# Clustered attention and two mixers: pair 1's raw rows fetched with pair 0's, another order of the set-up

## The chip, the cores and the metric

One core of one Trainium2 chip. The metric is the device time of one execution, in microseconds (us); a table below gives the runs. The engines are PE (matmul), PEld (its weight loads), DVE, ACT, POOL and SP; SP and ACT also issue DMAs, each on a queue of its own (SPq, ACTq in the rows).

## The reference

```python
q_assign = np.argmax(np.einsum('bhsd,hcd->bhsc', q_n, c_n), axis=-1)   # 16 clusters; k_assign likewise
mask = q_assign[:, :, :, None] == k_assign[:, :, None, :]
scores = np.where(mask, scale * np.matmul(q, k.transpose(0, 1, 3, 2)), -1e9)
attn = softmax(scores)                    # over the last axis
x = attn @ v                              # 2 batches, 8 heads, 768 rows, head size 64
# then two mixers on x (2, 768, 512):
#  u = x + (x^T U V)^T ; x = u + relu(u w1) w2          U: 768x32, w1: 512x2048
#  u = x + (relu(x^T T1) T2)^T ; out = u + relu(u w1) w2  T1: 768x256, w1: 512x1536
```

## The kernel before

The attention runs over 8 pairs (2 batches x 4 pairs of heads). A pair's q and k rows are a block of 128 partitions (two heads of 64, a = 0 and 1) by 768 positions, loaded raw into Rq and Rk. From them come a high part (rounded, Hq, Hk) and a low part (the rest), which DMAs stack into the operands qS and kS: "hi" (the high part), "lo" (the low part) and "mask", the rows that the cluster choice gives, so that one matmul adds scores and mask. `cross` (L250) issues the two DMAs of each stack that change partitions.

The cluster choice of a pair: PE multiplies the raw rows with the normalised centroids zc (`scores`), DVE transposes the result out of PSUM (`scores_out`, L198), then an argmax in steps arg0 (L206), arg1, arg2 (L219), arg3, arg4 (L229) and `mask_rows` (L232), on DVE or partly on POOL.

A pair has 12 tiles, 96 in all. Tile n takes, in `step`: the score matmuls of tile n+2 (`s_mm`, 4 matmuls into two PSUM banks), their row maximum on DVE (`s_max`, L292), the exponential on ACT (`s_exp`, L297), six PE transposes (`t_mm`, L314) and their evacuation (`t_out`, L319 or L321) into the blocks `pt`, and, from step 7 on, the products with v (`pv`). `ident` is the 128x128 identity. The order of the program on each engine is written out by hand: lists `mid`, `low`, `acts` and `late` say what else is issued in a step, and each engine works strictly in the order written. A DMA that has to wait stops those behind it on its queue.

All matmuls have line L73 (the helper `mm`), all roundings on ACT L78, the subtractions L85. Ahead of the loop stands `setup`: it loads the centroids (L390, L391), pair 0's raw rows (L392, L393) and v (L186), normalises the centroids (L412 to L421), transposes them (L423, copies L425), rounds pair 0's q and k for a = 0 and 1 (L435 to L440, low part of q L438), and does pair 0's cluster choice and masks (L442 to L452); then it loads pair 1's raw rows into Rq and Rk (`load_pair`, L444), rounds them (`q_hi`, `k_hi`), stacks them, does tiles 0 and 1's scores and maxima, pair 1's cluster scores and low parts (L461 to L466). The rest of pair 1's choice follows in steps 0 to 5, its masks in step 6. `load_uv` (L474) loads U and V of the first mixer in step 3; ACT takes U's magnitude (L96, `uv`) in step 11, V's in step 13. Behind the attention come the mixers, almost all PE work.

Of the kernel before, what the change touches and what calls it, by code (L numbers as in the profile page):

```python
# [10 lines left out]
F32R = mybir.dt.float32r  # L11
# [4 lines left out]
ALU = mybir.AluOpType  # L16
# [8 lines left out]
def tile_cluster_attention__then__two_mixers(  # L25
# [49 lines left out]
    def rnd(eng, o, i, scale=1.0):  # L75

        if eng is act:
            act.activation(o, i, AF.Copy, scale=scale)  # L78
        elif eng is dve and scale == 1.0:
            dve.tensor_copy(o, i)  # L80
        else:
            eng.tensor_scalar(out=o, in0=i, scalar1=scale, scalar2=1.0, op0=ALU.mult, op1=ALU.mult)

    def sub(eng, o, a, b):
        eng.tensor_tensor(out=o, in0=a, in1=b, op=ALU.subtract)  # L85
# [90 lines left out]
    wcl = const.tile([P, 16], BF16, name="wcl")  # L176
    msk = const.tile([P, 2], F32, name="msk")

    def load_pair(g, eng=sp):
        b, p = divmod(g, NPAIR)  # L180
        eng.dma_start(Rq, qT[b, p])
        eng.dma_start(Rk, kT[b, p])

    def load_v(g):
        b, p = divmod(g, NPAIR)
# [1 line left out]

    held = {}

    def scores(g):  # L190
        p = g % NPAIR
        held["sc"] = bk = ring()
        for qd in range(4):
            src = (Rq, Rk)[qd // 2]
            mm(ps[32 * qd : 32 * qd + 32, bk, 0:HS], zc[:, ts(p, 32)], src[:, ts(qd % 2, HS)], True, True)

    def scores_out():
        dve.transpose(out=am1, in_=ps[:, held["sc"], 0:HS])  # L198

    v1 = am1.rearrange("p (g c) -> p g c", c=16)  # L200
    v2 = am2.rearrange("p (g c) -> p g c", c=16)
# [29 lines left out]
    def mask_rows(eng):  # L231
        eng.tensor_scalar(out=om, in0=ohT, scalar1=msk[:, 0:1], scalar2=msk[:, 1:2], op0=ALU.add, op1=ALU.mult)  # L232

    def q_hi():
        rnd(act, Hq.bitcast(F32R), Rq, 0.125)

    def k_hi():
        rnd(act, Hk.bitcast(F32R), Rk)

    def q_lo(eng, o):  # L240
        eng.scalar_tensor_tensor(out=o.bitcast(F32R), in0=Rq, scalar=0.125, in1=Hq, op0=ALU.mult, op1=ALU.subtract)

    def k_lo(eng, o):
        sub(eng, o.bitcast(F32R), Rk, Hk)

    def rows(a):
        m, x = 64 * a, 64 * (1 - a)
# [4 lines left out]
        for i in range(2):  # L252
            eng.dma_start(o[x, 1 - i, :], src[m.start + 32 * i : m.start + 32 * i + 32])

    def stack(g, a, what, eng, Lq=Rq, Lk=Rk):
        q, k = f32(qS[g % NST][a]), f32(kS[g % NST][a])
        m, _, y = rows(a)
        if what == "hi":
            eng.dma_start(q[m, :, :], Hq[m].unsqueeze(1).to_broadcast([64, 2, S]))
            eng.dma_start(k[m, 1, :], Hk[m])  # L260
            cross(k, Hk, a, eng)
        elif what == "lo":
            eng.dma_start(k[m, 0, :], Lk[m])
            cross(q, Lq, a, eng)
        else:
            e = eng if type(eng) is tuple else (eng, eng)
            for h in range(2):
                e[h].dma_start(q[y, 0, ts(h, HS)], om[32 * h + 16 * a : 32 * h + 16 * a + 16])
                e[1 - h].dma_start(k[y, 0, ts(h, HS)], om[64 + 32 * h + 16 * a : 80 + 32 * h + 16 * a])
# [34 lines left out]
    def ring():  # L304

        banks.append(banks.pop(0))
        return banks[-1]
# [78 lines left out]
    def setup():  # L386
        with tc.tile_pool(name="tmp", bufs=1) as tmp:
            cc = tmp.tile([P, 2, D], F32, name="cc")
            tiny = tmp.tile([P, 1], F32, name="tiny")
            act.dma_start(cc[:, 0, :], cen)  # L390
            sp.dma_start(cc[:, 1, :], cen)  # L391
            sp.dma_start(Rq, qT[0, 0])  # L392
            act.dma_start(Rk, kT[0, 0])  # L393
            load_v(0)
            make_identity(nc, ident)
            dve.memset(zc, 0.0)
            for t in (qS, kS):
                for i in range(NST):
                    (dve, pool)[i].memset(f32(t[i][1])[32:64], 0.0)
            wi = tmp.tile([P, 16], F32, name="wi")  # L400
            pool.iota(wi, pattern=[[-1, 16]], base=16, channel_multiplier=0, allow_small_or_imprecise_dtypes=True)
            dve.memset(msk[0:64, 0:1], 0.0)
            dve.memset(msk[0:64, 1:2], 1.0)
            dve.memset(msk[64:128, 0:1], -1.0)
            dve.memset(msk[64:128, 1:2], BIG)


            sq = tmp.tile([P, D], F32, name="sq")
            n2 = tmp.tile([P, 1], F32, name="n2")
            n1 = tmp.tile([P, 1], F32, name="n1")  # L410
            nr = tmp.tile([P, 1], F32, name="nr")
            dve.tensor_tensor(out=sq, in0=cc[:, 0, :], in1=cc[:, 0, :], op=ALU.mult)  # L412
            dve.tensor_reduce(out=n2, in_=sq, axis=AX.X, op=ALU.add)
            dve.tensor_scalar(out=n2, in0=n2, scalar1=2.0 ** -100, scalar2=None, op0=ALU.max)
            act.activation(n1, n2, AF.Sqrt)
            dve.reciprocal(nr, n1)
            dve.tensor_tensor(out=nr, in0=nr, in1=n2, op=ALU.mult)
            dve.tensor_tensor(out=n1, in0=n1, in1=nr, op=ALU.add)
            dve.tensor_scalar(out=n1, in0=n1, scalar1=0.5, scalar2=1e-6, op0=ALU.mult, op1=ALU.add)
            dve.reciprocal(nr, n1)  # L420
            dve.tensor_scalar(out=cc, in0=cc, scalar1=nr, scalar2=None, op0=ALU.mult)  # L421
            ct = ps[:, 6, 0:P]
            pe.transpose(ct, cc.rearrange("p a d -> p (a d)"), ident)  # L423
            for a in range(2):
                dve.tensor_copy(  # L425
                    zc[64 * a : 64 * a + 64, :].rearrange("p (h j) -> p h j", j=32)[:, :, 16 * a : 16 * a + 16],
                    ct[64 * a : 64 * a + 64].rearrange("p (h j) -> p h j", j=32)[:, :, 16 * a : 16 * a + 16],
                )
            dve.tensor_copy(wcl, wi)

            l = p32[0]
            for a in range(2):
                m, _, _ = rows(a)
                q, k = qS[0][a], kS[0][a]
                rnd(act, q[m], Rq[m].unsqueeze(1).to_broadcast([64, 2, S]), 0.125)  # L435
                rnd(act, k[m, 1, :], Rk[m])
                sub(pool, k[m, 0, :], Rk[m], f32(k[m, 1, :]))
                dve.scalar_tensor_tensor(out=l[m].bitcast(F32R), in0=Rq[m], scalar=0.125, in1=f32(q[m, 0, :]), op0=ALU.mult, op1=ALU.subtract)  # L438
                cross(f32(k), f32(k[:, 1, :]), a, (act, sp)[a])
                cross(f32(q), l, a, sp)  # L440
            act.activation(tiny, n1, AF.Exp, scale=0.0)
            scores(0)  # L442
            scores_out()
            load_pair(1)  # L444
            arg0()
            arg1(dve)
            arg2()
            arg3(dve)
            arg4()
            mask_rows(dve)  # L450
            for a in range(2):
                stack(0, a, "mask", (act, sp))  # L452
            q_hi()
            k_hi()
            for a in range(2):
                stack(1, a, "hi", sp)
            s_mm(0)
            s_mm(1)
            s_max(0)
            s_max(1)  # L460
            scores(1)  # L461
            scores_out()
            q_lo(dve, Rq)
            k_lo(pool, Rk)
            for a in range(2):
                stack(1, a, "lo", sp)  # L466


    x_ = xn[:, 1].rearrange("p a b c -> p (a b c)")
# [100 lines left out]
    for g in range(G):  # L570
        s0 = NTT * g
        for h in range(2):
            s = s0 + 2 * NT * h + 4 * NT + 1
            at(mid, s, lambda q=2 * g + h: merge(q))
            at(late, s, lambda q=2 * g + h: merge_out(q))
        n, s1 = g + 1, s0
        if 2 <= n < G:
            at(late, s1 - 8 if n > 2 else 1, lambda g=n: load_pair(g))
            at(low, s1 - 3, lambda g=n: scores(g))
            at(acts, s1 - 5, q_hi)  # L580
            at(acts, s1 - 3, k_hi)
            for s, f in ((-3, scores_out), (-2, arg0), (-1, lambda: q_lo(dve, Rq)),
                         (-1, lambda: arg1(pool)), (-1, lambda: k_lo(pool, Rk)), (3, arg2), (3, lambda: arg3(pool)),
                         (5, arg4), (5, lambda: mask_rows(pool))):
                at(late, s1 + s, f)
            for what, s in (("hi", -2), ("lo", 1), ("mask", 7)):
                for a in range(2):
                    at(late, s1 + s, lambda g=n, a=a, w=what: stack(g, a, w, sp))
        if n < G:
            at(late, s1 + 6 if n > 1 else 4, lambda g=n: load_v(g))  # L590
# [6 lines left out]
    for t in range(NS):  # L597
# [5 lines left out]

        at(mid, s, za)
        at(late, s if s == 69 else s + 1, lambda t=t: zadd_out(0, t, held["za"]))
    for s, f in ((0, arg0), (1, lambda: arg1(pool)), (2, arg2), (3, lambda: arg3(pool)), (4, arg4), (5, lambda: mask_rows(pool))):
        at(late, s, f)
    for a in range(2):
        at(late, 6, lambda a=a: stack(1, a, "mask", sp))
    at(late, 3, load_uv)  # L610
    for i, s0, ss in ((0, 11, (12, 12, 12, 12)), (1, 13, (14, 16, 18, 20))):
        at(acts, s0, uv[i][0])
        for f, s in zip(uv[i][1:], ss):
# [360 lines left out]
```

## Time and profile before

| | us |
|---|---|
| median of 3 runs | 769.07 |
| lowest, highest | 767.74, 770.06 |
| the profiled execution | 767.95 |
| its span, first to last instruction | 766.2 |
| PE busy | 738.7 (96%) |
| DVE, ACT, POOL busy | 467.1, 310.1, 166.4 |

The times in rows are us from the start of the span, taken from one profiled execution. A busy PE isn't PE at its peak, since matmuls are pipelined. The page's row of granted clock shows full speed for all 40 slices; the durations in the first 23 us show another pace, so of those the durations are read.

### The profile page before, as it was taken

Reading aid. Unit: us, or ns where it says so; the run is one execution under the profiler, and the core shown is the slowest. Engines: PE = TensorE matmul, PEld = TensorE weight load, DVE = VectorE, ACT = ScalarE, POOL = GpSimd, SP = SyncE. Lnnn points to the kernel's source line nnn. Section 1 sums busy time; section 2 is a strip of 40 time slices with the busy share of each in tenths; the row PEclk is TensorE's granted clock in tenths of the full one; section 3 lists DMA queues with packets and bytes.
Section 4 is the critical chain, followed back from the end, with each engine's and each line's share of the span. In section 5 each row is a group of like instructions: output and inputs, shape, how many; then the busy total and the mean of one; then the engine's idle time right before and its main releaser. Section 6 shows DMA issues by size and latency. Waiting matters only on the chain.

```text
span 766.2 us, 10466 instructions
## 1 busy us (share of the span) xinstructions
PE 738.7 (96%) x3845; PEld 582.1 (76%) x3845; DVE 467.1 (61%) x689; ACT 310.1 (40%) x565; POOL 166.4 (22%) x147
## 2 busy tenths in 40 slices
PE   1899999999999999999999999999999999999998
PEld 0667766766666688888888888888888888888886
DVE  6778988877777366875758587666675432122113
ACT  3777877867776343332232324323232311111010
POOL 3321432421310122321322122125211410000000
PEclk9999999999999999999999999999999999999999
DMA  5886777875311344753632699967885647555652
GB/s 152 191 185 185 179 186 188 243 183 134 87 63 55 112 165 151 287 193 138 220 131 89 222 346 368 337 238 259 283 286 215 214 144 274 192 192 195 243 192 83
DMA packets 51714, 149.38 MB, mean 195 GB/s; under 512 B 7792, under 2 KB 15984, under 8 KB 49616
## 3 DMA queue, kind: packets, MB, share of 16 engines
q1 hardware_dynamic: 51152, 148.01, 59.7%
q10 hardware_dynamic: 512, 0.72, 0.3%
q8 instruction: 30, 0.49, 0.3%
q14 instruction: 20, 0.16, 0.1%
HBM read 97.32 MB, written 32.51 MB: 169 GB/s over the span
## 4 chain that ended last, share of the span: by engine, by line
PE 92%; DVE 3%; DMA 2%; ACT 2%; issue 1%; SPq 0%; ACTq 0%; DVEq 0%
PE ps L73 82%; PE ps L314 7%; DVE nm L292 1%; DMA xn<-in_U_dram 1%; ACT p L297 1%; ACT qk L78 1%; PE ps L377 1%; PE ps L822 1%; PE ps L334 1%; DMA sq__81<-in_qT_dram 1%; DMA qk<-om 0%; SPq L476 0%; DVE u_sb L100 0%; DVE xn L373 0%; DVE qk L85 0%
## 5 line engine op out<-in xcount | busy, mean ns | idle before, releaser
L727 DVE SCALAR_TENSOR_TENSOR gl<-ps,gh 128x512 fp32r<-128x512 f32 x84 | 58.0, 691 | 209.6 <-ACT gh L726 209.6
L73 PE MATMUL ps<-gh,qk 128*128 128x512 f32 x544 | 179.6, 391 | 0.1
L726 ACT ACTIVATE gh<-ps 128x512 fp32r<-128x512 f32 x84 | 50.2, 598 | 312.9 <-PE ps L73 311.5
L73 PE MATMUL ps<-qk 112*128 112x384 f32 (+2 forms) x456 | 110.8, 370 | 13.0 <-DMA qk<-om 10.3
L73 PEld LDWEIGHTS ps<-gh,qk 128*128 128x128 f32 x544 | 102.1, 188 | 21.6 <-issue 0.5
L292 DVE TENSOR_REDUCE nm<-ps 128x1 f32<-128x768 f32 x96 | 91.8, 956 | 41.5 <-PE ps L73 38.8
L73 PEld LDWEIGHTS ps<-qk 112*128 112x128 f32 (+1 forms) x456 | 77.2, 192 | 44.5 <-issue 20.7
L73 PE MATMUL ps<-gl,qk 128*128 128x512 f32 x272 | 106.1, 390 | 0.0
L85 POOL TENSOR_TENSOR qk<-c__77,qk 128x512 fp32r<-128x512 f32 x40 | 54.9, 1381 | 197.0 <-ACT qk L78 169.1
L297 ACT ACTIVATE p<-ps,nm 128x768 f32<-128x768 f32 x96 | 86.6, 902 | 7.4 <-DVE nm L292 6.8
L314 PE MATMUL ps<-ident,p 128*128 128x128 f32 x576 | 82.1, 275 | 2.6 <-DVE z L360 0.6
L314 PEld LDWEIGHTS ps<-ident,p 128*128 128x128 f32 x576 | 67.6, 140 | 12.8 <-ACT p L297 2.6
L73 PE MATMUL ps<-u2h,qk 128*128 128x512 f32 x224 | 73.9, 391 | 0.0
L73 PE MATMUL ps<-pt,vr 128*64 128x384 f32 x384 | 72.1, 498 | 0.0
L321 ACT COPY pt<-ps 128x512 f32<-128x512 f32 x96 | 56.1, 584 | 35.1 <-PE ps L314 34.7
L73 PEld LDWEIGHTS ps<-gl,qk 128*128 128x128 f32 x272 | 51.1, 188 | 10.2
L73 PE MATMUL ps<-u1h,qk 128*128 128x512 f32 x160 | 52.6, 390 | 0.0
L100 DVE TENSOR_SCALAR c__77<-c__77 128x512 f32<-128x512 f32 (+2 forms) x47 | 49.1, 1045 | 0.8 <-ACT c__77 L96 0.7
L73 PEld LDWEIGHTS ps<-u2h,qk 128*128 128x128 f32 x224 | 42.1, 188 | 8.6
L109 DVE SCALAR_TENSOR_TENSOR c__77<-c__76,c__77 128x512 int32<-128x512 int32 (+2 forms) x47 | 43.4, 923 | 1.5
L106 DVE SCALAR_TENSOR_TENSOR c__77<-c__76,c__77 128x512 int32<-128x512 int32 (+2 forms) x47 | 43.5, 925 | 1.1
L73 PE MATMUL ps<-u2l,qk 128*128 128x512 f32 x112 | 43.6, 390 | 0.0
(146 smaller groups left out, 1017.0 us busy)
## 6 DMA issues: line engine op xcount, KB each, us to landing
qk<-scr_b SPq DMA_DIRECT2D x72, 512.0 KB, 4.2
c__76<-in_wa_dram SPq DMA_DIRECT2D x16, 1024.0 KB, 4.8
qk<-scr_a SPq DMA_DIRECT2D x32, 512.0 KB, 7.6
c__76<-in_wb_dram SPq DMA_DIRECT2D x24, 512.0 KB, 5.1
scr_b<-qk SPq DMA_DIRECT2D x24, 512.0 KB, 4.2
scr_a<-wx SPq DMA_DIRECT2D x16, 512.0 KB, 2.9
scr_a<-qk SPq DMA_DIRECT2D x16, 512.0 KB, 2.7
qk<-sq__81 SPq DMA_DIRECT2D x14, 384.0 KB, 4.0
```

What stands on the lines that cost most here:

```text
L73: pe.matmul(o, lhsT=l, rhs=r, start=start, stop=stop, **kw)
L78: act.activation(o, i, AF.Copy, scale=scale)
L85: eng.tensor_tensor(out=o, in0=a, in1=b, op=ALU.subtract)
L100: dve.tensor_scalar(out=dst, in0=dst, scalar1=2.0 ** -15, scalar2=122879.9921875, op0=ALU.max, op1=ALU.min)
L106: dve.scalar_tensor_tensor(out=d, in0=lo, scalar=29, in1=d, op0=ALU.logical_shift_right, op1=ALU.bitwise_or)
L109: dve.scalar_tensor_tensor(out=d, in0=hi, scalar=-0x40000000, in1=d, op0=ALU.bitwise_and, op1=ALU.bitwise_or)
L292: dve.tensor_reduce(out=nm[:, n % 4 : n % 4 + 1], in_=ps[:, b0 : b0 + 2, 0:HS], axis=AX.XY, op=ALU.max, negate=True)
L297: act.activation(p32[n % NP32].rearrange("p (j k) -> p j k", j=2), ps[:, b0 : b0 + 2, 0:HS], AF.Exp, bias=nm[:, n % 4 : n % 4 + 1], accum_ ...
L314: pe.transpose(ps[:, tb[j], ts(i, P)], p32[n % NP32][:, ts(c, P)], ident)
L321: act.copy(o, ps[:, tb[j], :])
L726: act.activation(gh, o, AF.Relu)
L727: dve.scalar_tensor_tensor(out=gl, in0=o, scalar=0.0, in1=f32(gh), op0=ALU.max, op1=ALU.subtract)
```

## The change

- Pair 1's raw rows are loaded right behind pair 0's, q on SP's queue and k on ACT's, ahead of v, into four blocks of `pt` that no tile uses until tile 6 (`raw1`). The functions that read raw rows take the blocks as an argument.
- All four memsets of qS and kS rows are POOL's.
- The crossings of k of pair 0, a = 0, are issued by SP instead of ACT. Of pair 0's a = 1 the low parts of q and k (`low_q(1)`, `low_k(1)`) come behind the masks on DVE; the low part of k was POOL's.
- Pair 1's cluster scores are multiplied right after pair 0's; pair 1's rounding stands on ACT ahead of the load of the exponential's table; pair 1's transpose, arg0, arg1 and the low part of k stand before tile 0's maximum.
- `busy(n)` gives PE n transposes of the identity into bank 6 that nothing reads: 44 behind the cluster scores, 12 behind tile 1's scores.
- In the loop: the low part of pair 1's q in step 0, arg2 in step 1, arg3 and arg4 in step 2 and the mask rows in step 3, all on DVE; its "lo" stacks in step 1 and masks in step 3; pair 2's raw rows in step 3 instead of 1, `load_uv` in step 6 instead of 3.

```diff
+    raw = Rq, Hq, Rk, Hk
+    raw1 = tuple(pt[:, 2 * NBL * P + i * S : 2 * NBL * P + (i + 1) * S] for i in range(4))
+
-    def load_pair(g, eng=sp):
+    def load_pair(g, x=raw, engs=(sp, sp)):
         b, p = divmod(g, NPAIR)
-        eng.dma_start(Rq, qT[b, p])
-        eng.dma_start(Rk, kT[b, p])
+        engs[0].dma_start(x[0], qT[b, p])
+        engs[1].dma_start(x[2], kT[b, p])
...
             act.dma_start(Rk, kT[0, 0])
+            load_pair(1, raw1, (sp, act))
             load_v(0)
             make_identity(nc, ident)
             dve.memset(zc, 0.0)
-            for t in (qS, kS):
-                for i in range(NST):
-                    (dve, pool)[i].memset(f32(t[i][1])[32:64], 0.0)
+            for i in range(NST):
+                for t in (qS, kS):
+                    pool.memset(f32(t[i][1])[32:64], 0.0)
...
-            l = p32[0]
+            l = p32[3]
+
+            def low_q(a):
+                m, _, _ = rows(a)
+                dve.scalar_tensor_tensor(out=l[m].bitcast(F32R), in0=Rq[m], scalar=0.125, in1=f32(qS[0][a][m, 0, :]), op0=ALU.mult, op1=ALU.subtract)
+                cross(f32(qS[0][a]), l, a, sp)
+
+            def low_k(a, eng):
+                m, _, _ = rows(a)
+                sub(eng, kS[0][a][m, 0, :], Rk[m], f32(kS[0][a][m, 1, :]))
+
+            def busy(n):
+                for i in range(n):
+                    pe.transpose(ps[:, 6, ts(i % 4, P)], ident, ident)
+
             for a in range(2):
                 m, _, _ = rows(a)
                 q, k = qS[0][a], kS[0][a]
                 rnd(act, q[m], Rq[m].unsqueeze(1).to_broadcast([64, 2, S]), 0.125)
                 rnd(act, k[m, 1, :], Rk[m])
-                sub(pool, k[m, 0, :], Rk[m], f32(k[m, 1, :]))
-                dve.scalar_tensor_tensor(out=l[m].bitcast(F32R), in0=Rq[m], scalar=0.125, in1=f32(q[m, 0, :]), op0=ALU.mult, op1=ALU.subtract)
-                cross(f32(k), f32(k[:, 1, :]), a, (act, sp)[a])
-                cross(f32(q), l, a, sp)
+                if a == 0:
+                    cross(f32(k), f32(k[:, 1, :]), a, sp)
+                    low_q(0)
+                    low_k(0, pool)
+                else:
+                    cross(f32(k), f32(k[:, 1, :]), a, sp)
+            scores(0)
+            scores(1, raw1)
+            busy(44)
+            q_hi(raw1)
+            k_hi(raw1)
             act.activation(tiny, n1, AF.Exp, scale=0.0)
-            scores(0)
-            scores_out()
-            load_pair(1)
+            scores_out(0)
             arg0()
             arg1(dve)
             arg2()
...
             for a in range(2):
                 stack(0, a, "mask", (act, sp))
-            q_hi()
-            k_hi()
+            low_q(1)
+            low_k(1, dve)
             for a in range(2):
-                stack(1, a, "hi", sp)
+                stack(1, a, "hi", sp, raw1)
+            scores_out(1)
+            arg0()
+            arg1(pool)
+            k_lo(pool, raw1)
             s_mm(0)
             s_mm(1)
+            busy(12)
             s_max(0)
             s_max(1)
-            scores(1)
-            scores_out()
-            q_lo(dve, Rq)
-            k_lo(pool, Rk)
-            for a in range(2):
-                stack(1, a, "lo", sp)
...
-            at(late, s1 - 8 if n > 2 else 1, lambda g=n: load_pair(g))
+            at(late, s1 - 8 if n > 2 else 3, lambda g=n: load_pair(g))
...
-    for s, f in ((0, arg0), (1, lambda: arg1(pool)), (2, arg2), (3, lambda: arg3(pool)), (4, arg4), (5, lambda: mask_rows(pool))):
+    for s, f in ((0, lambda: q_lo(dve, raw1)), (1, arg2), (2, lambda: arg3(dve)), (2, arg4), (3, lambda: mask_rows(dve))):
         at(late, s, f)
-    for a in range(2):
-        at(late, 6, lambda a=a: stack(1, a, "mask", sp))
-    at(late, 3, load_uv)
+    for what, s in (("lo", 1), ("mask", 3)):
+        for a in range(2):
+            at(late, s, lambda a=a, w=what: stack(1, a, w, sp, raw1))
+    at(late, 6, load_uv)
```

## Rows read from the trace of the kernel before

**Rows 1.** The page: chain by engine; PE's transposes (count, busy, mean ns).
```profile
PE 92%; DVE 3%; DMA 2%; ACT 2%; issue 1%; SPq 0%; ACTq 0%; DVEq 0%
...
L314 PE MATMUL ps<-ident,p 128*128 128x128 f32 x576 | 82.1, 275 | 2.6 <-DVE z L360 0.6
```
**Rows 2.** Chain of waits, 0 to 60 us, in time: start, us, what.
```profile
1.18 4.65 DMA sq__81<-in_qT_dram
...
5.86 2.23 ACT qk L78 x2
...
8.10 0.61 ACTq L253
...
37.16 6.62 DMA xn<-in_U_dram
```
**Rows 3.** Timeline, 0 to 25: start, us, engine, line, operation [idle before <- releaser].
```profile
1.65 0.43 SPq L186 DMA_DIRECT2D vr<-in_v_dram  x1
...
2.95 1.34 DVE L399 MEMSET qk<- 32x1536 f32 x1 [0.27 <-issue]
...
4.53 0.23 DVE L412 TENSOR_TENSOR sq<-cc 128x64 f32<-128x64 f32 x1
...
7.32 0.46 DVE L425 COPY zc<-ps 64x64 f32<-64x64 f32 x2 [0.59 <-PE ps L423]
```
**Rows 4.** DMA issues before 2 us: transfer, queue, count, KB, us to landing.
```profile
cc<-in_cen_dram ACTq DMA_DIRECT2D x1, 32.0 KB, 1.9
...
sk__82<-in_kT_dram ACTq DMA_DIRECT2D x1, 384.0 KB, 4.9
...
vr<-in_v_dram SPq DMA_DIRECT2D x1, 384.0 KB, 5.5
```
**Rows 5.** Timeline, 10 to 21: ACT and DVE from the rounding to the masks.
```profile
10.91 0.95 DVE L438 SCALAR_TENSOR_TENSOR p<-sq__81,qk 64x768 fp32r<-64x768 f32 x1 [2.08 <-ACT qk L78]
11.63 1.28 ACT L441 ACT_TABLE_LOAD   x1
...
11.90 0.58 DVE L198 STREAM_TRANSPOSE am<-ps 128x384 f32<-128x384 f32 x1
...
14.40 0.55 DVE L219 TENSOR_REDUCE amx<-am 128x24 f32<-128x384 bf16 x1
...
16.19 0.48 DVE L232 TENSOR_SCALAR om<-ohT,msk 128x384 f32<-128x384 bf16 x1
...
19.45 0.84 ACT L78 ACTIVATE sq__81<-sq__81 128x768 fp32r<-128x768 f32 x1 [6.32 <-DMA qk<-om]
```
**Rows 6.** Timeline, 6 to 25: PE.
```profile
6.83 0.45 PE L423 MATMUL ps<-ident,cc 128*128 128x128 f32 x1 [6.83 <-DVE cc L421]
...
8.46 0.85 PE L73 MATMUL ps<-sq__81,zc 128*32 128x384 f32 x2
...
19.03 2.90 PE L73 MATMUL ps<-qk 112*128 112x384 f32 x8 [9.70 <-DMA qk<-om]
...
23.16 0.98 PE L73 MATMUL ps<-qk 112*128 112x384 f32 x4
...
23.98 1.04 PE L314 MATMUL ps<-ident,p 128*128 128x128 f32 x8
```
**Rows 7.** Timeline, 23 to 33: DVE, from q's low part to tile 6's maximum.
```profile
23.84 2.34 DVE L241 SCALAR_TENSOR_TENSOR sq__81<-sq__81 128x768 fp32r<-128x768 f32 x1
...
26.10 0.94 DVE L292 TENSOR_REDUCE nm<-ps 128x1 f32<-128x768 f32 x1
...
28.29 0.68 DVE L319 COPY pt<-ps 128x512 f32<-128x512 f32 x1
...
32.66 0.95 DVE L292 TENSOR_REDUCE nm<-ps 128x1 f32<-128x768 f32 x1
```
**Rows 8.** Timeline, 45 to 48: PE at tile 12, ACT at U's magnitude.
```profile
45.53 0.95 PE L73 MATMUL ps<-qk 112*128 112x384 f32 x4 [0.55 <-DMA qk<-om]
...
47.44 0.38 ACT L96 ACTIVATE u_sb<-xn 128x192 f32<-128x192 f32 x1
```

## What was predicted before the changed kernel ran

> **What bounds the kernel now.** I read the page first, then the chain of waits in order of time, then the timeline of the first 48 us engine by engine, then the DMA issues with their time to landing. The page says that PE is 92% of the chain that ended last [rows 1]. So what happens late can't be shortened by this change, and what is gained early, before PE is full, should stay gained: behind it stands PE work that only moves forward. The place to look is the set-up: PE has a transpose and the cluster scores, then sits idle for 9.70 us until a mask DMA lands, and starts its first score matmuls at 19.03 [rows 6].
>
> The chain up to there [rows 2]: q lands (issued 1.18, 4.65 later), ACT rounds q and k of half a=0 (2.23), ACT then *issues* two DMAs (about 0.61 each), only after them rounds half a=1; DVE's L438 waits for that until 10.91, and the transpose of the cluster scores, L198, stands behind L438 on DVE and starts at 11.90 [rows 5]. The argmax from there to the end of the mask rows (L232, 16.19 + 0.48 = 16.67) takes 4.77. From there to PE's start are 2.36. PE had the scores done by 9.3; it isn't what L198 waits for [rows 6].
>
> **The change part by part.**
>
> *Memsets to POOL.* DVE writes two memsets, the second until 4.29, and begins the centroid norm at 4.53 without an idle gap, though the centroids were issued at about 0.7 and land 1.9 later [rows 3, 4]. With all four on POOL, DVE starts at about 2.65, 1.9 sooner, and the zc copies (7.32 + 0.46) end near 5.9. POOL gets 2.7 more and is free by about 6.9, before its first subtraction wants it. Scores of pair 0 then wait for k, which lands about 4.9 after its issue, near 6.1. This alone gains nothing on the path.
>
> *First loads.* Pair 1's raw rows go out on the two queues behind pair 0's and ahead of v. v, issued 1.65, behind q on the same queue, landed 5.5 later, at 7.15, some 1.3 after q [rows 2 to 4]: a queue's transfers land in their order, so some 1.3 us for another 384 KB. So q and k keep their place; pair 1's rows land by about 8, v a little later, and v is wanted some 30 us later. The lower bound is no cost. The upper one is that four blocks share alike and q lands when all have: two blocks more at 1.3, so 2 us or little over; I take none, since v behind q did not hold it back in that way.
>
> *ACT no longer issues.* The crossings of k go to SP. ACT rounds a=0 until 8.1, a=1 (another 2.23) until 10.3, pair 1's q and k (0.84 each) until 12.0, loads the table (1.28) until 13.3, and after the small exponential is free at 13.5 [rows 2, 5].
>
> *Argmax sooner.* DVE now does only half 0 of the low part first. ACT's q of a=0 is done at about 7.3 (2.23 less the 0.84 of a k); L438's work takes 0.95, so L198 starts at 8.3 rather than 11.90: 3.6 sooner. The scores (from zc's copies to 9.3 now, some 1.5 us at the slow clock [rows 3, 6]; here from 6.2) are ready by 7.8. The mask rows end at 16.67 - 3.6 = 13.1. But four of the eight mask DMAs are ACT's, and ACT is free at 13.5: that is what is late next. 13.5 + 2.36 gives a first score matmul at 15.9 instead of 19.03, a gain of 3.1. SP has three pairs of crossings ahead of the masks; at 0.61 each the last pair, ready at 10.3, is out by about 12, so SP isn't late. Half 1's low parts, two operations of 0.95 on DVE, and their crossings come behind the masks; they land near 19 and are first needed by tile 3, near 20.7.
>
> *Unread transposes on PE.* 44 of them stand between pair 1's scores (done near 9.3) and the first score matmul, 12 behind the second. Now eight take 1.04 and one by itself 0.27 (the page's mean), so (1.04 - 0.27) / 7 = 0.11 for one more, at the fast clock [rows 1, 6]. At the slow clock no row has a run of them: at least 0.11, at most the 0.45 of the lone one at 6.83; I take twice the fast price, 0.22, because the two levels (1.2 and 2.4 GHz) are a factor of two apart. PE ran slowly from 19.03 (eight score matmuls 2.90) and fast at 23.16 (four in 0.98): the rise lies in that stretch, in which PE worked without a gap. Here work begins with the scores at 6.2, and after as much of it PE would be fast by 10.4 at the latest: half a dozen transposes at 0.22, the rest at 0.11, about 5.5 in all, ending at 14.8, a microsecond before the masks land. So they cost nothing, and buy the first eight score matmuls at 1.95 instead of 2.90; the 12 behind them cost 1.3, hidden under the first row maximum and exponential.
>
> That is the place for a rule that speaks against the change. The Trainium skill, "TensorE: Matmul & The Clock Gate", Part 4 (PE-mode transpose), says that the full clock doesn't engage for transposes, since they don't count as PE work in the same way. The trace agrees with it only in part: transposes run at both paces here, 0.45 for the lone one and 0.27 in the loop by the page's mean, but no stretch of the trace is transposes alone. If the rule holds, the result is the first rival below.
>
> *Into the loop.* First score matmuls 15.9 to 16.9, maximum and exponential to 18.9; PE's own list, 1.95 of score matmuls and 1.3 of transposes, ends at 19.15. So tile 2's matmuls start at 19.2 instead of 23.16 (pair 1's scores no longer stand before them): 4.0 sooner.
>
> *DVE in steps 0 to 3.* Now the low part of q of pair 1 (2.34, beside POOL's subtraction) stands ahead of tile 2's maximum, which starts at 26.10 though its matmuls were done near 24.1 [rows 7]. That stall of 2 us goes: tile 2's maximum starts at about 20.15. But what is taken out of the set-up's end comes back behind it. Up to the maximum of tile 6 DVE does four maxima (0.95), two evacuations (0.68, L319), q's low part (0.95), and the rest of the argmax, which was partly POOL's: L219 to L232, 14.40 to 16.67 [rows 5], 2.27. Sum 3.8 + 1.36 + 0.95 + 2.27 = 8.4, with gaps 8.6. Tile 6's maximum starts near 28.75 where it was at 32.66: a gain of 3.9. DVE is the bound there, not PE. If POOL's subtraction overlaps q's low part, up to 1.4 is lost (2.34 against 0.95); I take none, as POOL has it queued right behind its share of the argmax, some 2 us before DVE gets there. From tile 7 on nothing is added, and PE fills with the second products.
>
> *Masks of pair 1.* They go out at step 3 instead of 6, ahead of the U and V loads, which move from 3 to 6. Now PE waits 0.55 for them at 45.53 [rows 8], since the mask issues on SP stood behind U, whose transfer took 6.62 [rows 2]. This wait goes: 0.55 more. Also moved: pair 2's raw rows, from step 1 to 3, still ahead of the masks on SP, and wanted at step 7.
>
> Sum: 3.9 + 0.55, about 4.5 us. The profiled execution took 767.95 (span 766.2 and 1.75 around it); less 4.5 that is 763.4. The median of the runs, 769.07, is 1.1 above it; the forecast for the median is **764.6**, with a range of its own of 763.0 to 766.2.
>
> **The rivals.**
> 1. *The transposes don't raise the clock* (slower than before). All 44 at 0.22 are 9.7, so PE reaches the first score matmul at 9.3 + 9.7 = 19.0, as now, and does eight of them in 2.90, 12 transposes in 2.6: tile 2 starts at 24.5, 1.3 later than now. Its maximum is then no earlier than now (26.1), DVE's 8.6 follow, so tile 6 is 2.0 later; the mask wait returns 0.55. About 1.4 slower: 770.5. It decides as soon as a transpose takes over (15.9 - 9.3) / 44 = 0.15 on average; each 0.023 beyond costs a microsecond. For it: no row shows a rise under transposes. Against it: real matmuls come before them, and they do run at the fast pace in the loop. Chance 0.2.
> 2. *U becomes the wait.* ACT takes U's magnitude at 47.44, and U landed at 43.8: 3.7 in hand [rows 2, 8]. With the loop 4.5 sooner and U issued no sooner than now, ACT would wait 0.8 to 1.5 in line before an exponential. Time 765.8. Against it: SP is free of pair 1's stacks some 4 us sooner. Chance 0.13.
> 3. *The extra loads slow the first ones.* q and k 2 us late: everything behind moves, gain 2.5, 766.6. Against it: v's landing. Chance 0.08.
> 4. The forecast: 0.57. The remaining 0.02: something unseen.
>
> **How the numbers follow.** A measurement of this kernel tells about 0.3%, or 2.3 us, from no change: faster means below 766.8, slower above 771.4. The forecast gives 0.54 of its 0.57 to faster, rival 2 0.11, rival 3 0.04: 0.69. Rival 1 gives 0.05 to slower; 0.06 with the rest. The remainder, 0.25, is no difference. The range runs from 762.8 (DVE less of a bound than I sum) to 769.6, which takes in rivals 2 and 3 and a part of the first, and leaves out some 0.17.
>
> **What would show it.** L198 at 8.3 and the mask rows done at 13.1; the first score matmul at 15.9, eight in under 2.0; tile 2's matmuls at 19.2; DVE without idle from tile 2 to tile 6; no mask wait at tile 12. Wrong, if the transposes are still 0.22 apart at 14 and PE goes from them to the scores with no gap, if pair 1's scores start late for want of their rows, or if ACT idles for U.

## The result

The changed kernel takes 761.48 us (median of 5 runs, 761.31 to 761.82) against 768.71 of the kernel before on the same chip (median of 5, 767.74 to 770.06): a ratio of 0.9907, 95% interval 0.9892 to 0.9921, so 7.2 us faster. On another chip, 761.65 against 767.66, 0.9925 (0.9912 to 0.9937), 6.0 us. The profiled executions are 766.2 and 759.7 us long, 6.5 apart. The forecast was 764.6 with a lowest of 762.8: right in direction and place, but 3.1 us too high. Some 2 of these are gain that it missed (4.5 forecast, 6.5 between the profiled executions). The other 1.1 it had added to get from the profiled execution to the median, and the changed kernel has none of it: its profiled execution took 761.48, too.

The page of the changed kernel, PE's busy time and the chain by engine, to be read against [rows 1]:

```profile
PE 744.7 (98%) x3901; PEld 587.8 (77%) x3901; DVE 465.3 (61%) x690; ACT 309.8 (41%) x565; POOL 164.1 (22%) x145
...
PE 91%; DVE 3%; ACT 2%; DMA 2%; SPq 1%; issue 1%; DVEq 0%; ACTq 0%
```

PE has 6 us more of busy time in a span 6.5 us shorter: the 56 unread transposes take 7.2 (44 in 5.75, 12 in 1.48), and the first eight score matmuls 1.1 less than before. The timeline of the set-up (start, us, engine, line, operation [idle before <- releaser]), against [rows 5, 6]:

```profile
8.22 0.58 DVE L201 STREAM_TRANSPOSE am<-ps 128x384 f32<-128x384 f32 x1
...
12.51 0.48 DVE L235 TENSOR_SCALAR om<-ohT,msk 128x384 f32<-128x384 bf16 x1
...
13.02 0.60 ACTq L272 DMA_DIRECT2D qk<-om  x1
13.09 0.20 ACT L467 ACTIVATE tiny<-n 128x1 f32<-128x1 f32 x1
...
9.26 1.71 PE L449 MATMUL ps<-ident 128*128 128x128 f32 x7
...
10.60 2.67 PE L449 MATMUL ps<-ident 128*128 128x128 f32 x22
...
15.37 1.77 PE L73 MATMUL ps<-qk 112*128 112x384 f32 x8 [0.35 <-DMA qk<-om]
...
18.50 0.98 PE L73 MATMUL ps<-qk 112*128 112x384 f32 x4
```

The cluster scores leave PSUM at 8.22 instead of 11.90, and PE starts its score matmuls at 15.37 instead of 19.03, eight in 1.77 instead of 2.90. Seven transposes take 1.71, 22 later ones 2.67: the spacing falls from 0.21 to 0.11 near 10.8, in the midst of the transposes. From tile 12 to the end the two kernels run in step, 6.4 to 6.6 us apart: everything is decided before. (In the table the last time of the forecast is 45.53 less the 4.45 of the prediction's sum.)

| start, us | before | forecast | after |
|---|---|---|---|
| transpose of the cluster scores (L198, now L201) | 11.90 | 8.3 | 8.22 |
| first score matmul | 19.03 | 15.9 | 15.37 |
| matmuls of tile 2 | 23.16 | 19.2 | 18.50 |
| row maximum of tile 2 | 26.10 | 20.15 | 19.58 |
| row maximum of tile 6 | 32.66 | 28.75 | 27.43 |
| matmuls of tile 12 | 45.53 | 41.1 | 38.99 |

### The profile page after: what moved, and what is told of

The parts are those of the page before. It is cut to its first block, busy times and chain, and to the rows that moved or that the text cites. A ratio compares the mean times of both kernels' runs of the same rounds, so it can differ in the third digit from the quotient of the medians.

```text
span 759.7 us, 10577 instructions
## 1 busy us (share of the span) xinstructions
PE 744.7 (98%) x3901; PEld 587.8 (77%) x3901; DVE 465.3 (61%) x690; ACT 309.8 (41%) x565; POOL 164.1 (22%) x145
## 4 chain that ended last, share of the span: by engine, by line
PE 91%; DVE 3%; ACT 2%; DMA 2%; SPq 1%; issue 1%; DVEq 0%; ACTq 0%
PE ps L73 82%; PE ps L318 7%; DVE nm L296 1%; ACT p L301 1%; PE ps L381 1%; PE ps L338 1%; PE ps L846 1%; DMA xn<-in_U_dram 1%; DMA sq__81<-in_qT_dram 1%; ACT qk L78 1%; SPq L273 0%; SPq L272 0%; DMA qk<-om 0%; SPq L499 0%; DVE xn L377 0%
## 5 line engine op out<-in xcount | busy, mean ns | idle before, releaser
L73 PEld LDWEIGHTS ps<-pt,vr 128*64 128x64 f32 x384 | 23.4, 136 | 26.3 <-issue 26.3
```

Source lines behind the costliest of these rows:

```text
L73: pe.matmul(o, lhsT=l, rhs=r, start=start, stop=stop, **kw)
```

## The experiments

Each ratio is to the kernel before on the same chip. Differences to the changed kernel are between profiled executions, or to its 761.5 us. Theory A and the rivals are those of the expectation that stands ahead of each result.

**No unread transposes.**

```diff
-            busy(44)
-            busy(12)
```

> The changed kernel without both groups of unread transposes. Theory A (they bring TensorE to its fast pace before the masks land): PE idles from 9.3 to 15.4, the first eight score matmuls are 0.32 apart and take about 2.9 us instead of 1.77, tile 2's row maximum starts at 20.2 to 20.7 instead of 19.58, and the time is 0.6 to 1.2 us above the changed kernel's 761.5. Rival B (the pace rises in the first score matmuls anyway, and the loss is absorbed by tile 12, where PE becomes the bound): tile 12 as in the changed kernel, within 0.3 us of it. Rival C (transposes don't raise the pace): same durations as in the changed kernel.

763.65 us, 0.9945 of the kernel before (0.9931 to 0.996); span 761.9, 2.2 above the changed kernel. PE's timeline:

```profile
15.50 2.90 PE L73 MATMUL ps<-qk 112*128 112x384 f32 x8 [5.97 <-DMA qk<-om]
19.19 1.65 PE L73 MATMUL ps<-qk 112*128 112x384 f32 x4 [0.79 <-ACT p L301]
20.63 1.91 PE L318 MATMUL ps<-ident,p 128*128 128x128 f32 x8
22.19 1.63 PE L73 MATMUL ps<-qk 128*128 128x384 f32 x4
...
24.33 1.01 PE L73 MATMUL ps<-qk 128*128 128x384 f32 x4
```

The slow pace lasts from 15.5 to past 23, not for eight matmuls alone. Tile 2's maximum is 1.4 later than in the changed kernel (20.94, past the 20.2 to 20.7 that was expected), tile 3's 2.2, tile 12's still 2.2 (42.27 against 40.07), and none of it comes back. Theory A, with twice the price it gave; the transposes are worth a third of the gain here.

**Transposes ahead of everything.**

```diff
+            busy(24)
             ct = ps[:, 6, 0:P]
```

> The changed kernel with 24 more unread transposes ahead of PE's first instruction, so that nothing but transposes runs on PE from 1.4 to about 6. Theory A (transposes alone raise the pace as matmuls do, some 4 us after PE begins to work): their spacing goes from 0.21 to 0.11 us between 5 and 6, and the cluster scores behind them run in 0.52 to 0.6 instead of 0.85 each. Rival (the rise at 10.8 in the changed kernel was due to the cluster scores): all 24 stay 0.21 apart, end at 6.5, and the cluster scores take 0.85.

One run, span 762.8. PE's timeline, and windows of it (stretch, length, PE busy, granted clock, DMA share, GB/s):

```profile
1.35 5.38 PE L429 MATMUL ps<-ident 128*128 128x128 f32 x24 [1.35 <-POOL ident masks.py:199]
...
7.49 0.52 PE L73 MATMUL ps<-sq__81,zc 128*32 128x384 f32 x2 [0.55 <-DVE zc L435]
...
16.21 2.13 PE L73 MATMUL ps<-qk 112*128 112x384 f32 x8 [1.78 <-DMA qk<-om]
18.15 2.76 PE L429 MATMUL ps<-ident 128*128 128x128 f32 x12
```

```profile
16.20:17.40 1.20, 1.19 (x6) 1.00 0.35 78
17.40:20.80 3.40, 3.40 (x17) 0.51 0.52 113
20.80:24.00 3.20, 3.08 (x22) 0.99 0.95 196
```

All 24 were at the slow pace, to 6.7, so the expected change within them didn't come; but the cluster scores, the first matmuls of another kind, started fast, 0.52 instead of the 0.85 of [rows 6]. PE had done nothing but transposes: they raise the clock.

The run shows a second thing, which was not expected. The 44 transposes, fast from the start, ended at 14.4, PE stood idle for 1.78, and a little later the granted clock was 0.51, the lower level, for 3.4 us in the midst of work. In the changed kernel the transposes end 0.35 before the masks land, and no fall follows. That the idle stretch brought the fall is not shown: it is one run, and in the kernel before PE stands idle longer, 1.98, and goes on at the full pace (granted clock 1.00 from there to 40):

```profile
28.12 0.98 PE L73 MATMUL ps<-qk 128*128 128x384 f32 x4 [1.98 <-ACT p L297]
28.94 1.04 PE L314 MATMUL ps<-ident,p 128*128 128x128 f32 x8
```

The kernel lost 3 us, and not by the clock alone. The 24 transposes hold back the cluster scores by 0.95 (7.49 against 6.54 in the changed kernel) and with them the mask rows by 0.9. Tile 2's maximum is 2.2 late, tile 12's 1.75; the rest comes behind tile 13, where ACT waits for U:

```profile
45.35 0.38 ACT L96 ACTIVATE u_sb<-xn 128x192 f32<-128x192 f32 x1 [2.58 <-DMA xn<-in_U_dram]
```

**Memsets back on DVE.**

```diff
-                    pool.memset(f32(t[i][1])[32:64], 0.0)
+                    (dve, pool)[i].memset(f32(t[i][1])[32:64], 0.0)
```

> The changed kernel with two of the four memsets back on DVE. The prediction called this part off the path taken alone. Theory A (with the argmax moved ahead, the cluster scores are what DVE waits for next): zc's copies end near 7.8, the cluster scores near 9.3, their transpose starts at 9.3 to 9.5 instead of 8.22, and the time rises by 0.9 to 1.3 us. Rival B (it stays off the path, as predicted for the part alone): no change beyond 0.2 us.

762.70 us, 0.9935 (0.9918 to 0.9951); span 760.9, 1.2 above the changed kernel.

```profile
9.43 0.58 DVE L201 STREAM_TRANSPOSE am<-ps 128x384 f32<-128x384 f32 x1 [0.60 <-PE ps L73]
...
16.71 1.66 PE L73 MATMUL ps<-qk 112*128 112x384 f32 x8
```

DVE waits for the scores now: theory A. A part that the prediction priced at nothing taken alone (it was not run alone) carries 1.2 us of the whole, since the other part moved what stood before it.

**The first crossing back on ACT.**

```diff
-                    cross(f32(k), f32(k[:, 1, :]), a, sp)
+                    cross(f32(k), f32(k[:, 1, :]), a, act)
```

> The changed kernel with the first crossing of k issued by ACT again. Theory A (ACT's list is the path to the masks, level with DVE's): half 1 is rounded 1.2 us later, ACT's mask issues start at 14.2 to 14.4 instead of 13.02, the first score matmul at 16.4 to 16.7 instead of 15.37, and the time rises by 0.8 to 1.3 us. Rival B (ACT's four issues aren't those that land last): under 0.3 us.

761.51 us, 0.9919 (0.9904 to 0.9934): no difference to the changed kernel, and theory A is refuted. ACT's timeline, its computations and its DMA issues, with one issue of SP's:

```profile
11.49 1.58 ACT L78 ACTIVATE pt<-pt 128x768 fp32r<-128x768 f32 x2
...
13.01 0.52 ACTq L272 DMA_DIRECT2D qk<-om  x1
13.09 1.28 ACT L467 ACT_TABLE_LOAD   x1
13.56 0.59 SPq L272 DMA_DIRECT2D qk<-om  x1
13.57 0.85 ACTq L273 DMA_DIRECT2D qk<-om  x1
14.38 0.20 ACT L467 ACTIVATE tiny<-n 128x1 f32<-128x1 f32 x1
```

The mask issues stand behind the table load and the small exponential in the program, and the first goes out before both, while ACT is still rounding (to 13.07): it didn't wait for computations of ACT's ahead of it that it doesn't need. So ACT keeps to the order written in its computations, not in its DMA issues. The converse doesn't hold: behind the crossing's issues the next rounding starts 1.31 idle. In the changed kernel's chain of waits the first score matmul is released by a mask of SP's, issued at 13.56 and 1.81 on its way.

**U and V in step 3.**

```diff
-    at(late, 6, load_uv)
+    at(late, 3, load_uv)
```

> The changed kernel with U and V asked for in step 3, behind the masks that now stand in step 3 too, instead of step 6. Theory A (SP is the limit there and reaches these loads behind the masks either way): under 0.2 us. Rival B (the order against v's next block matters: v is behind U and V then, its transfer and U's change places): ACT's wait of 1.14 for U at 42.2 shrinks by 0.5 or more, but the time moves by less than 0.3, since that wait lies beside PE's work.

761.47 us, 0.9919 (0.9904 to 0.9933): level, though ACT's wait for U is gone (it takes U at 40.96 instead of 42.16). That wait of 1.14 in the changed kernel costs nothing, even if the profile's chain of waits runs through it.

**The low part of pair 1's q in the set-up.**

```diff
+            q_lo(dve, raw1)          # behind s_max(1)
-    for s, f in ((0, lambda: q_lo(dve, raw1)), (1, arg2), ...
+    for s, f in ((1, arg2), ...
```

> The changed kernel with the low part of pair 1's q on DVE right behind tile 1's maximum, where DVE now idles 1.30 us for PE, instead of behind tile 2's. Theory A (DVE is the bound from tile 2 to tile 6, and what it is late there stays): tile 2's maximum at 19.6 to 19.9, tile 3's at 20.9 instead of 21.75, tile 6's 0.5 to 1.0 earlier, and the time 0.5 to 0.9 us below the changed kernel's. Rival B (pair 2's raw rows or PE bind by tile 9): tile 6 is earlier, tile 12 is not, and the time is within 0.2 us of the changed kernel's.

761.82 us, 0.9922 (0.9907 to 0.9937): not faster. DVE and ACT:

```profile
26.85 0.95 DVE L296 TENSOR_REDUCE nm<-ps 128x1 f32<-128x768 f32 x1
```

```profile
30.73 0.59 ACT L325 COPY pt<-ps 128x512 f32<-128x512 f32 x1 [0.46 <-DMA qk<-pt]
32.29 0.84 ACT L78 ACTIVATE sq__81<-sq__81 128x768 fp32r<-128x768 f32 x1 [0.97 <-DMA sq__81<-in_qT_dram]
```

Tile 6 is 0.58 earlier, tile 10 0.23 later (35.15 against 34.92): ACT waits for pair 2's q. What DVE gains between tiles 2 and 6, a DMA takes at tile 10.

**Pair 2's raw rows in step 1.**

```diff
-            at(late, s1 - 8 if n > 2 else 3, lambda g=n: load_pair(g))
+            at(late, s1 - 8 if n > 2 else 1, lambda g=n: load_pair(g))
```

> The changed kernel with pair 2's raw rows asked for in step 1, ahead of pair 1's low stacks on SP, as the kernel before has it, instead of step 3. Theory A (ACT's wait of 0.43 for these rows at 31.9 stands in line before an exponential): that wait goes and the time falls by 0.2 to 0.5 us. Rival B (PE is the bound from tile 7 on, and this wait is behind its work): the wait goes, tile 12's start and the time stay within 0.2 us.

762.90 us, 0.9937 (0.992 to 0.9953); 1.5 us slower in span than the changed kernel, against both theories.

```profile
33.08 0.59 ACT L325 COPY pt<-ps 128x512 f32<-128x512 f32 x1 [2.27 <-DMA qk<-pt]
33.56 0.85 ACT L78 ACTIVATE sq__81<-sq__81 128x768 fp32r<-128x768 f32 x1
```

The wait for q is gone, and a longer one stands in its place: the blocks that held pair 1's rows are wanted by tile 6's transposes, and the low stacks that still read them now stand behind pair 2's load. The idle blocks are idle only until then.

**Pair 2's q rounded later, too.** q_low_in_setup, and `at(acts, s1 - 5, q_hi)` becomes `s1 - 3` for pair 2.

> The changed kernel with the low part of pair 1's q behind tile 1's maximum (as in q_low_in_setup) and, besides, pair 2's q rounded on ACT in step 9 instead of 7. Theory A (what sets tile 10 is ACT standing in line for pair 2's q, which lands near 32): ACT's wait of 0.97 at 32.29 goes, tile 10's maximum starts at 34.2 to 34.6 instead of 35.14, tile 12's at 39.3 to 39.7 instead of 40.07 in the changed kernel, and the time is 0.4 to 0.8 us below the changed kernel's. Rival B (the next DMA, or the stack for pair 2, takes its place): tile 12 within 0.2 of the changed kernel's.

763.42 us (762.64 to 764.55), 0.9945 (0.993 to 0.996). Tile 12's maximum is at 39.80 instead of 40.07, just short of theory A's 39.3 to 39.7; then the next DMA holds ACT, and the time rises instead of falling, as rival B feared:

```profile
43.65 0.37 ACT L96 ACTIVATE u_sb<-xn 128x192 f32<-128x192 f32 x1 [2.90 <-DMA xn<-in_U_dram]
```

**The transposes alone, in the kernel before.**

```diff
             scores(0)
+            for i in range(70):
+                pe.transpose(ps[:, 6, ts(i % 4, P)], ident, ident)
             scores_out()
```

> The kernel before with 70 unread transposes behind pair 0's cluster scores, nothing else. Fast pace from 13 on, so the first eight score matmuls take 1.8 instead of 2.9 and tile 2 starts about 1.5 earlier. Theory A (what sets tile 10 in the kernel before is the landing of pair 2's q at 37.9, which comes from SP's list and not from PE): tile 10 moves by at most 0.5 us and the time by 0 to 0.7. Rival B (the fast pace is worth the same here as in the changed kernel): tile 10 and the time move by about 2.

767.11 against 767.56 us, 0.9991 (0.9982 to 1.0). Tile 2's maximum is 1.7 earlier than in the kernel before, tile 9's still 1.7, tile 10's 0.9, tile 12's 0.3.

```profile
45.22 0.94 PE L73 MATMUL ps<-qk 112*128 112x384 f32 x4 [1.13 <-DMA qk<-om]
```

PE's wait for pair 1's masks, 0.55 in [rows 8], has become 1.13. Here the same fast pace is worth 0.3 in the trace and 0.45 in the medians, where it is worth 2.2 in the changed kernel: theory A in the time, though tile 10 moved by more than the 0.5 it allowed. That came from a DMA and not from PE: pair 2's q, asked for at 33.96 instead of 33.71, landed 3.1 us after that instead of 4.2, and ACT rounds it at 37.10 instead of 38.00.

**Pair 2's q later, in the kernel before.** `at(acts, s1 - 5, q_hi)` becomes `s1 - 3` for pair 2, nothing else.

> The kernel before with pair 2's q rounded on ACT in step 9 instead of 7, nothing else. Theory A (ACT stands in line for that landing, 1.06 idle at 38.0, and PE behind it): tile 10's maximum starts 0.4 to 0.9 earlier than 41.25; the masks of pair 1, landing near 45.5, then hold tile 12, so tile 12 moves by under 0.2 and so does the time. Rival B (the wait is behind PE's work): tile 10 doesn't move.

767.76 against 767.56 us, 1.0 (0.999 to 1.001). Tile 10's maximum stays at 41.25, but in this execution tile 9 was 0.3 late, so it tells little of the wait itself (from tile 9 to 10 it is 3.2 instead of 3.5); tile 12 is unchanged, as both would have it.

**Both DMA waits opened, in the kernel before.**

```diff
-            at(acts, s1 - 5, q_hi)
+            at(acts, s1 - 5 if n > 2 else s1 - 3, q_hi)
-    at(late, 3, load_uv)
-    for i, s0, ss in ((0, 11, (12, 12, 12, 12)), ...
+    at(late, 7, load_uv)
+    for i, s0, ss in ((0, 15, (16, 16, 16, 16)), ...
```

> The kernel before with pair 2's q rounded in step 9 instead of 7, U and V asked for in step 7 (behind pair 1's masks) instead of 3, and U converted in steps 15 and 16 instead of 11 and 12. Theory A (in the kernel before, tile 12 is held by the masks behind U, and tile 10 by pair 2's q): tile 12's maximum starts 0.4 to 0.8 earlier than 46.59 and the time falls by as much. Rival B (the late tiles are bound by PE): under 0.2.

767.44 against 767.78 us, 0.9993 (0.9983 to 1.0003). Tile 12's maximum is at 46.05 instead of 46.59, but in the trace, of one of the longest of ten runs (766.71 to 768.44), the end is no earlier: ACT waits 2.4 for pair 3's q instead.

> The same with 70 unread transposes behind pair 0's cluster scores. Theory A (the fast pace was worth 0.45 in the kernel before because those two DMA waits took the rest): now tile 12 is 1.5 to 2.3 earlier than in the kernel before, and the time is 1.5 to 2.3 lower. Rival B (something else took it): 0.4 to 1.0.

With the transposes as well, tile 12's maximum is at 44.10, 1.95 earlier than without them and 2.5 earlier than in the kernel before (1.5 to 2.3 was expected), and the spans are 764.7 and 766.6. PE meets no mask wait:

```profile
43.02 0.98 PE L73 MATMUL ps<-qk 112*128 112x384 f32 x4
```

The timed runs lie between 765.2 and 771.5 (ratio 0.999, 0.9972 to 1.0009), so the time itself is unclear; by the traces the fast pace gives 1.9 to 2.2 where these two waits are out of the way, and 0.3 where the masks hold tile 12.

**A version with three of these moves, and with four.** In the changed kernel: q's low part in the set-up, pair 2's q in step 9, U and V in step 3, U converted in steps 15 and 16; the fourth moves the mixer's first weight block from step 8 to 17.

> The changed kernel with the low part of pair 1's q behind tile 1's maximum, pair 2's q rounded in step 9, U and V ahead of v's next block (step 3), and U converted in steps 15 and 16. If the waits named so far are all that stands between tile 2 and tile 14, tile 12's maximum starts at 39.8 instead of 40.07, tile 14's at 44.3 instead of 44.57, and the time is 0.2 to 0.4 us below the changed kernel's. If another DMA takes their place, it is level or above.

760.48 against 767.78 us, 0.9912 (0.9897 to 0.9927), some 1.0 below the changed kernel's 761.5 on other chips. The trace is of the longest of its four runs, 761.59 with a span of 759.8; the other three took 760.27 to 760.54. In it tile 12's maximum is at 39.84, tile 16's 1.2 earlier than in the changed kernel, and by tile 22 it is all gone:

```profile
60.56 0.84 ACT L78 ACTIVATE sq__81<-sq__81 128x768 fp32r<-128x768 f32 x1 [1.83 <-DMA sq__81<-in_qT_dram]
```

Whether the three shorter runs met this wait is not known.

> The changed kernel as it is, beside the two that follow on the same chip: 761.5, or 0.991 of the kernel before.

> The changed kernel with the first 1 MB block of the mixer's weights asked for in step 17 instead of 8; it is used in step 23. Theory A (in the changed kernel, too, ACT waits at step 19 for pair 3's q, 0.54 at 59.9, and that load stands behind pair 2's stacks, which share the DMA engines with this block): pair 3's q is there in time, the wait of 0.54 goes, and the time is 0.3 to 0.6 below the changed kernel's. Rival B (PE is the bound from tile 13 on): under 0.2.

> three_moves with this block in step 17 as well. Theory A (three_moves was 1.2 earlier than the changed kernel at tile 16 and lost it in a wait of 1.83 for pair 3's q at 60.6): most of that wait goes, tile 24 starts 0.8 to 1.6 earlier than the changed kernel's 68.38, and the time is 0.8 to 1.6 below it. Rival B: level, within 0.3.

On one chip, beside 767.66 of the kernel before: the changed kernel 761.65 (0.9925), the weight block alone 762.32 (0.993, 0.9918 to 0.9942), all four moves 760.54 (0.9908, 0.9893 to 0.9923). The block alone brings nothing: pair 3's q is there, but U is 1.6 late for ACT. Tile 18's maximum is 0.35 later than in the changed kernel and tile 22's as much, so the wait of 0.54 for q, which stood between them and is gone, had been hidden by PE's work: rival B. With four moves tile 24's maximum is at 67.32 instead of 68.38, and the span is 758.6, 1.1 shorter. This version beats both kernels, by 1.1 us over the changed one. That it needs the fourth move is not shown: three alone took 760.48 on their chip, and the two were not run side by side.

No run takes out pair 1's early load or the new place of the argmax by itself. What they bring is read from the traces; if the shares add up, it is the 3 us that no_transposes (2.2) and memsets_on_dve (1.2) leave of 6.5.

## Why the prediction was off, step by step

**Right:** where the time was to come from, that ACT's list and DVE's order held the cluster choice (8.3 forecast, 8.22), that q, k and pair 1's rows land in time, the rise of the clock among the first transposes (10.4 forecast, near 10.8), the hidden 44, and no mask wait at tile 12. That the gain stays to the end came out right, too, but not for the reason given (point 3), so it was luck in part. The rival of the unraised clock is refuted by transposes_first and by the changed kernel itself. The rule on transposes in the Trainium skill, "TensorE: Matmul & The Clock Gate", Part 4, does not hold for these f32 transposes: they alone brought the 0.85 of the cluster scores down to 0.52.

**Mis-sized or wrong,** in the order of the sum; of the 2 us of gain that it missed, 0.6 lie in point 1 and 0.75 each in points 2 and 3:

1. *ACT as the last of the masks, 0.5.* The step put the mask issues behind ACT's table load, at 13.5. They went at 13.02, as soon as the mask rows were done (12.99), and crossing_on_act shows that ACT's computations don't hold them. The first score matmul came at 15.37 instead of 15.9, and tile 2's maximum 0.6 earlier than forecast.

2. *DVE's sum up to tile 6, 8.6 us, 0.75 too long.* The changed kernel's DVE, from tile 2's maximum to tile 6's:

```profile
19.58 0.96 DVE L296 TENSOR_REDUCE nm<-ps 128x1 f32<-128x768 f32 x1 [1.30 <-PE ps L73]
...
20.46 1.37 DVE L244 SCALAR_TENSOR_TENSOR pt<-pt 128x768 fp32r<-128x768 f32 x1
...
21.75 0.94 DVE L296 TENSOR_REDUCE nm<-ps 128x1 f32<-128x768 f32 x1
...
23.68 0.94 DVE L296 TENSOR_REDUCE nm<-ps 128x1 f32<-128x768 f32 x1
...
24.54 0.54 DVE L229 TENSOR_TENSOR am<-am,amx 128x384 bf16<-128x384 bf16 x1
25.11 0.58 DVE L232 STREAM_TRANSPOSE ohT<-am 128x384 bf16<-128x384 bf16 x1
25.61 0.92 DVE L296 TENSOR_REDUCE nm<-ps 128x1 f32<-128x768 f32 x1
...
27.43 0.95 DVE L296 TENSOR_REDUCE nm<-ps 128x1 f32<-128x768 f32 x1
```

The operations are those of the sum, with q's low part at 1.37 rather than 0.95 (POOL's subtraction ran beside it until 21.01; the forecast had named this and taken none of it). Their durations add up to 8.58. But ten of the eleven starts come 0.06 to 0.08 before the record of the one ahead ends (23.68 + 0.94 is 24.62; the next starts at 24.54), where the sum had added a gap; only L232, which reads what L229 wrote, starts 0.03 after it. The eleven take 7.85.

3. *What holds tiles 10 to 12 in the kernel before: 0.55 in the sum, 1.3 in the trace.* This is the step that failed in kind. The forecast carried the gain at tile 6 to the end, with DVE as the bound until PE is full, because what is gained early "should stay gained". q_low_in_setup refutes this: 0.58 gained there is lost by tile 10. (A delay does stay: the 2.2 of no_transposes at tile 3 are there to the end.) Between tile 6 and 12 the kernel before is held by DMAs. One is the masks (the 0.55 that was counted): they land behind U and v's next block, which stand ahead of them on SP's queue. Of v's block and the first mask (issued at 37.63 and 38.22), the us to landing:

```profile
vr<-in_v_dram SPq DMA_DIRECT2D x1, 384.0 KB, 7.3
qk<-om SPq DMA_DIRECT2D x1, 24.0 KB, 6.9
```

The other is ACT's rounding of pair 2's q in step 7, which the forecast named as "wanted at step 7" and did not price; q is asked for at 33.71 and lands 4.2 later. Before and after:

```profile
38.00 0.84 ACT L78 ACTIVATE sq__81<-sq__81 128x768 fp32r<-128x768 f32 x1 [1.06 <-issue]
```

```profile
31.93 0.84 ACT L78 ACTIVATE sq__81<-sq__81 128x768 fp32r<-128x768 f32 x1 [0.43 <-DMA sq__81<-in_qT_dram]
```

before_transposes shows how much these hold back: 1.7 us at tile 9 shrink to 0.3 at tile 12. In the changed kernel the whole list of DMAs is earlier as well (pair 1's load is out of it, its stacks start at 16.78 instead of 20.32, pair 2's q is asked for at 28.71 instead of 33.71), and so the waits do not eat what PE and DVE gain. The share of each is not settled: with both waits opened tile 6 to tile 12 takes 13.0 in the kernel before instead of 13.9, in the changed kernel 12.6. Of the last 0.4, the traces show tile 10's maximum in the kernel before waiting for the transposes behind its matmuls, and not so in the changed one (before, then after); why was not tried.

```profile
41.25 0.96 DVE L292 TENSOR_REDUCE nm<-ps 128x1 f32<-128x768 f32 x1 [1.93 <-PE ps L314]
```

```profile
34.92 0.96 DVE L296 TENSOR_REDUCE nm<-ps 128x1 f32<-128x768 f32 x1 [1.22 <-PE ps L73]
```

4. *The clock, 1 us for the first eight matmuls, 2.2 in no_transposes.* It was priced by those eight alone; without the transposes the slow pace reaches to tile 3. The price of the part was too low, but the sum lost nothing by it, since its terms had the fast pace: from the first score matmul to tile 2's it had 3.25 where 3.13 were measured.

5. *From the profiled execution to the median, 1.1.* The sum gave 763.4; the forecast added the 1.1 by which the median of three runs of the kernel before lay above its profiled execution. Those three spread from 767.74 to 770.06. On the five chips of the experiments the median of the kernel before is 767.56 to 767.96, level with the profiled 767.95: the term was the spread of three runs.

**U as the wait,** the second rival: ACT does wait 1.14 for it in the changed kernel,

```profile
42.16 0.38 ACT L96 ACTIVATE u_sb<-xn 128x192 f32<-128x192 f32 x1 [1.14 <-DMA xn<-in_U_dram]
```

as long as that rival said, but PE has work meanwhile and the time is the same without it (uv_at_3). In q_low_and_q_hi_later, where it is 2.90, the span is 1.4 longer than the changed kernel's.

## What to carry to other kernels

A gain early in a pipelined kernel is worth what the next scheduled DMA leaves of it: before carrying it on, go through every wait for a DMA up to the point where one engine is full, and price how far each moves by itself. A wait that is hidden now can be the bound as soon as another is taken away; here that happened in q_low_in_setup, q_low_and_q_hi_later and before_gates_open, and only moving several together gained. Unread work on PE paid where it raised the clock before the real work came and held none of it up; the 24 transposes of transposes_first held up the cluster scores, and the kernel lost. And what lies between one profiled execution and the median of three runs is no term of a sum until more runs show it.

## What the runs showed of the hardware

- Transposes raise TensorE's clock: after 24 of them 0.21 apart and nothing else, the first matmuls ran in 0.52 instead of 0.85 (transposes_first). In the same run, once, 1.78 us of idle with the clock up were followed by 3.4 us at a granted 0.51, while PE worked; 1.98 us of idle in the kernel before were not. What brought the fall stays open.
- A DMA issue on ACT goes out ahead of ACT's unfinished computations that it doesn't depend on (13.01, with a table load at 13.09 that precedes it in the program); computations behind it wait until it is issued (1.31; both in crossing_on_act).
- In the changed kernel ten of eleven DVE operations from 19.58 to 27.43 start 0.06 to 0.08 us before the record of the one ahead ends; the eleventh, L232, reads what the one ahead wrote and starts 0.03 after it. In the cluster choice from 8.22 to 12.99, where each operation reads what the one ahead wrote, all seven start 0.03 to 0.04 after.
- In the kernel before, a mask of 24 KB that stood on SP's queue behind a 384 KB load took 6.9 us to land, at 45.1, just after that load (44.9); the last mask, issued at 44.94, took 1.8.
